# Windowed attention softmax over 128 merged columns in a three-stage float32 kernel

## The chip, the core and the metric

The kernel runs on one core of one Trainium2 chip. The metric is the device time of one execution in microseconds (us). The engines are TensorE (PE; PEld is its weight load), VectorE (DVE), ScalarE (ACT), GpSimd (POOL) and SyncE (SP), which here only issues DMAs.

## The reference, cut to what matters

Attention over 2 batches, 8 heads, 576 positions of 64 numbers, with a causal window of 128 keys; its output, as 1152 tokens of 512 numbers, goes through a layer of four experts and then through a second network with a cosine in it.

```python
rel = pos[:, None] - pos[None, :]
bias = slopes[:, None, None] * (-np.abs(rel).astype(np.float32))[None, :, :]
mask = (rel >= 0) & (rel < 128)
scores = np.where(mask, scale * np.matmul(q, k.transpose(0, 1, 3, 2)) + bias[None], -1000000000.0)
attn = np.exp(scores - np.max(scores, axis=-1, keepdims=True))
attn = attn / (np.sum(attn, axis=-1, keepdims=True) + 1e-09)
x = np.matmul(attn, v)                      # then laid out as [1152, 512]
for e in range(4):                          # p: domain_probs over their sum
    out += p[:, e:e + 1] * (np.maximum(x @ w1[e], 0.0) @ w2[e])
h = out @ w_in
return (h * np.cos(h)) @ w_out
```

## The kernel before

The order of all instructions on each engine is written out by hand: loops in Python yield pieces, and the pieces are queued in the order in which the loops call them. Each engine takes its own queue strictly in that order.

**Attention** comes first. A unit is a batch and a block of queries (one of 64, four of 128); `attention` takes each unit in two halves of four heads, so there are 20 steps, numbered k = 0 to 19. Step k queues the scores of its own half (`att_scores`: TensorE into `s_ps`, a VectorE add, scale and minimum per head at L358, a ScalarE exponential per head at L363), the reciprocal of step k-1 (`att_sums`, with a GpSimd add of 1e-9 at L372), one job of `weights()`, the transposes of step k-3 with the two copies `pt` out of PSUM (L411 VectorE, L413 ScalarE), the normalisation of step k-1 on GpSimd (L379), and the products with the values of step k-4 (L429, into `x_ps`). After a second half the result is split into a high and a low part on ScalarE and VectorE. A query block sees its own 128 keys and the 128 of the block ahead, so scores, exponentials and normalisation run over 256 columns, of which the mask `bm` leaves 128. From step 12 on, matmuls of the first layer (`plain`, L561) are put between. Jobs of `weights()` split the weights of the next group of 512 hidden features into a high part (ScalarE, L155 and L184) and a low part (GpSimd, L130).

**Groups** follow: eight for the experts, four for the second network. A group is two `pair` products (L533), `layer2` products (L627) and four `plain` products for the next group. Between them `run` calls `jobs`, `advance` (the cosine and its split), `cv` (which converts the second network's weights, given as 8-byte words, through `cr` and `cv` tiles at L224 to L251) and `move` (which makes the seven transformed operands of the pair products out of the tokens, `transform`). In the last expert group (`turn`) the results are transposed (`flip`, named f0 to f8) to become the second network's input.

At the very start four matmuls on zeros (`WARM`, L683) run while the first keys are on their way. The keys of the first batch lie in the tile `xk`, whose first part later becomes `xf`.

Of the kernel before, what the change touches and what calls it, by code (L numbers as in the profile page):

```python
# [49 lines left out]
def tile_kernel(ctx, tc, qT, kT, v, probs, w1, w2, w_in, w_out, out):  # L50
# [21 lines left out]
    ptp = ap("ptp", bufs=4)  # L72
# [7 lines left out]
    scr = ppool.tile([128, 4, 256], F32, name="scr", tag="p")  # L80
    bm = mkp.tile([128, H, 256], BF16, name="bm")

    def constants():
        rel_i, rel, msk = scr[:, 0].bitcast(I32), scr[:, 1], scr[:, 2]
        nc.gpsimd.iota(rel_i, pattern=[[-1, 256]], base=WIN, channel_multiplier=1)
        nc.vector.tensor_copy(rel, rel_i)
        nc.gpsimd.memset(msk, 0.0)
        big = -8.0e9
        nc.gpsimd.affine_select(
            out=msk, in_=msk, pattern=[[-1, 256]], compare_op=ALU.is_ge, fill=big,  # L90
            base=WIN, channel_multiplier=1,
        )
# [5 lines left out]
        for h in range(H):
            slope = 2.0 ** (-8.0 * (h + 1) / H)
            nc.vector.scalar_tensor_tensor(  # L100
                out=bm[:, h, :], in0=rel, scalar=-8.0 * slope, in1=msk,
                op0=ALU.mult, op1=ALU.add,
            )
        make_identity(nc, ident)


    k_t, q_t, v_t = {}, {}, {}

    def load_unit(b, i):
# [13 lines left out]
        q_t[b, i], v_t[b, i] = qt, vt  # L123

# [23 lines left out]
    def weights():  # L148
# [17 lines left out]
        def first_sums(g, j):  # L166

            raw, w = raws[j], w_t[1, g, j]
            a11, a12 = raw[:, 0:2, 0:128], raw[:, 2:4, 0:128]
            a21, a22 = raw[:, 0:2, 128:256], raw[:, 2:4, 128:256]  # L170
            sm = ssp.tile([128, 4, 2, 128], F32, name="sm", tag="sm")
            nc.gpsimd.tensor_tensor(out=sm[:, 0], in0=a21, in1=a22, op=ALU.add)
            sub(nc.gpsimd, sm[:, 1], sm[:, 0], a11)
            sub(nc.gpsimd, sm[:, 2], a11, a21)
            sub(nc.gpsimd, sm[:, 3], a12, sm[:, 1])
            loads_ahead()
            yield
            yield from two_parts(nc.gpsimd, w[:, 0, 1], w[:, 1, 1], sm.rearrange("p s m f -> p (s m f)"))
# [156 lines left out]

    def att_scores(u, g):
# [15 lines left out]
        den = stp.tile([128, 4], F32, name="den", tag="den")
        rec = stp.tile([128, 4], F32, name="rec", tag="rec")
        for m in range(2):
            for hh in range(2):
# [3 lines left out]
                    out=p[:n, k, :wid], in0=ps[hh][:n, m, :wid], in1=bm[:n, h, c0 : c0 + wid],  # L359
# [4 lines left out]
                    out=p[:n, k, :wid], in_=p[:n, k, :wid], func=AF.Exp, scale=-1.0,  # L364
                    bias=nmax[:n, k : k + 1], accum_out=den[:n, k : k + 1],
                )
        state[u, g] = p, den, rec, wid

    def att_sums(u, g):
        n = UNITS[u[1]][1]  # L370
        p, den, rec, wid = state[u, g]
        nc.gpsimd.tensor_scalar(out=den[:n], in0=den[:n], scalar1=1e-9, scalar2=None, op0=ALU.add)  # L372
        nc.vector.reciprocal(out=rec[:n], in_=den[:n])  # L373

    def att_normalise(u, g):
        n = UNITS[u[1]][1]
        p, den, rec, wid = state[u, g]
        for s in (slice(0, 2), slice(2, 4)):
            nc.gpsimd.tensor_tensor(  # L379
                out=p[:n, s, :wid], in0=p[:n, s, :wid],  # L380
                in1=rec[:n, s].unsqueeze(2).to_broadcast([n, 2, wid]), op=ALU.mult,
            )
        state[u, g] = p

    def key_blocks(i):
        o = 0
        for j in ([i - 1] if i else []) + [i]:
            yield j, o, UNITS[j][1]
            o += UNITS[j][1]

    def att_transpose(u, g):
        p = state[u, g]
        n = UNITS[u[1]][1]
        blocks = list(key_blocks(u[1]))
        pT = []
        for m in range(2):
            tp = ps_t.tile([128, 2, 2, 128], F32, name="t_ps", tag="t_ps")
            pt = ptp.tile([128, 2, 2, 128], F32, name="pt", tag="pt")
            for bi, (j, o, ln) in enumerate(blocks):
                for hh in range(2):  # L400
                    nc.tensor.transpose(  # L401
                        tp[:ln, bi, hh, :n], p[:n, 2 * m + hh, o : o + ln], ident[:n, :n]
                    )
            lens = [ln for j, o, ln in blocks]
            if len(set(lens)) == 1:
                sl = [(slice(0, lens[0]), slice(0, len(blocks)))]
            else:
                sl = [(slice(0, lens[k]), slice(k, k + 1)) for k in range(2)]
            for a, bb in sl:
                if m == 0:  # L410
                    nc.vector.tensor_copy(pt[a, bb, :, :n], tp[a, bb, :, :n])  # L411
                else:
                    nc.scalar.activation(out=pt[a, bb, :, :n], in_=tp[a, bb, :, :n], func=AF.Copy)  # L413
            pT.append(pt)
        state[u, g] = pT

    def att_pv(u, g):
        b, i = u
        s0, n = UNITS[i]
        pT = state.pop((u, g))  # L420
        blocks = list(key_blocks(i))
# [3 lines left out]
        for m in range(2):  # L425
            for bi, (j, o, ln) in enumerate(blocks):
                for hh in range(2):
                    h = 4 * g + 2 * m + hh
                    nc.tensor.matmul(  # L429
                        xt[64 * hh : 64 * hh + 64, 2 * g + m, :n],  # L430
                        v_t[b, j][:ln, 64 * h : 64 * h + 64],
                        pT[m][:ln, bi, hh, :n],
                        start=(bi == 0), stop=(bi == len(blocks) - 1),
                    )
# [243 lines left out]
    with tc.manual_schedule():  # L678

        warm = ppool.tile([128, 4, 256], F32, name="warm", tag="p")  # L680
        nc.vector.memset(warm[:, 0], 0.0)
        for _ in range(WARM):
            nc.tensor.matmul(  # L683
                ps1.tile([128, 512], F32, name="o_ps", tag="o_ps")[:, :256],
                warm[:, 0, :128], warm[:, 0], start=True, stop=True,
# [5 lines left out]
        def fill(k, s):  # L691
# [7 lines left out]
            if s == 0 and 4 <= k < 18:  # L699
# [26 lines left out]
    def steps(g):  # L726
# [17 lines left out]
        if g > 0:  # L744
            yield layer2(g, 1), 2, 2 * turn, 2
# [5 lines left out]
        njobs = 0 if last else 2 if turn else 5 if early else 9  # L751
        if g == 0:
            njobs += 1
        for k, o in enumerate(order):
            more = min(njobs, 2 if g == 0 and k == 0 else 1)
            if isinstance(o, int):
                assert not any(c > 0 for c, _ in chains)
                yield layer2(g, o), 2, more, 2 if k in (1, 4, 7) else 1 if k < 9 else 0
# [3 lines left out]
            elif not last:  # L762
                yield plain(g + 1, int(o[1])), 2, more, 2
            njobs -= more

    def run(groups):
        for g in groups:
            for step, stages, njobs, ncv in steps(g):
                next(step)
                for _ in range(stages):  # L770
# [5 lines left out]
                move(2)  # L776
# [7 lines left out]
    with tc.manual_schedule():  # L784
        run(range(NG1 - 1))
# [45 lines left out]
```

## Time and profile before

| | us |
|---|---|
| median of 3 runs | 676.09 (674.96 to 679.61) |
| the profiled execution | 675.06 |
| its span, first to last instruction | 673.3 |
| TensorE busy in the span | 648.1 |
| VectorE, GpSimd, ScalarE busy | 420.4, 372.4, 336.7 |

The span leaves 1.76 us of the execution outside. Busy times are sums over stages that differ, so they only tell which engine has little room on the whole.

### The profile page before, as it was taken

Reading aid. Unit: us, or ns where it says so; the run is one execution under the profiler, and the core shown is the slowest. Engines: PE = TensorE matmul, PEld = TensorE weight load, DVE = VectorE, ACT = ScalarE, POOL = GpSimd, SP = SyncE. Lnnn points to the kernel's source line nnn. Section 1 sums busy time; section 2 is a strip of 40 time slices with the busy share of each in tenths; the row PEclk is TensorE's granted clock in tenths of the full one; section 3 lists DMA queues with packets and bytes.
Section 4 is the critical chain, followed back from the end, with each engine's and each line's share of the span. In section 5 each row is a group of like instructions: output and inputs, shape, how many; then the busy total and the mean of one; then the engine's idle time right before and its main releaser. Section 6 shows DMA issues by size and latency. Waiting matters only on the chain.

```text
span 673.3 us, 9797 instructions
## 1 busy us (share of the span) xinstructions
PE 648.1 (96%) x3516; PEld 569.5 (85%) x3516; DVE 420.4 (62%) x821; ACT 336.7 (50%) x768; POOL 372.4 (55%) x376
## 2 busy tenths in 40 slices
PE   8879999979999999999999999999899999999997
PEld 5667789878898898998998998988788998998976
DVE  5645674587866858659669663455675464564562
ACT  6868744245334334344343251246675675675660
POOL 3987737517538147357166174194458749649540
PEclk7989999999999999999999999999999999999999
DMA  8135101553625504526325322011001200201002
GB/s 259 40 121 164 32 1 34 183 159 87 198 76 156 173 32 156 173 57 207 104 102 202 126 48 78 32 63 33 1 32 33 77 17 32 93 2 47 34 31 93
DMA packets 39728, 60.41 MB, mean 90 GB/s; under 512 B 5632, under 2 KB 22016, under 8 KB 39680
## 3 DMA queue, kind: packets, MB, share of 16 engines
q1 hardware_dynamic: 39680, 59.80, 27.7%
q8 instruction: 27, 0.44, 0.3%
q14 instruction: 21, 0.17, 0.1%
HBM read 49.04 MB, written 10.75 MB: 89 GB/s over the span
## 4 chain that ended last, share of the span: by engine, by line
PE 75%; DVE 8%; ACT 6%; POOL 5%; issue 3%; DMA 2%; SPq 0%; ACTq 0%; DVEq 0%; POOLq 0%
PE o_ps L627 38%; PE o_ps L533 20%; PE o_ps L561 13%; POOL p L379 2%; DVE u L505 2%; ACT r L503 2%; PE s_ps L346 2%; DMA cr<-w_in 2%; ACT u L502 2%; PE x_ps L429 2%; POOL hpair L130 1%; PE t_ps L401 1%; DVE o_ps L576 1%; DVE u L511 1%; DVE c L576 1%
## 5 line engine op out<-in xcount | busy, mean ns | idle before, releaser
L627 PE MATMUL o_ps<-w2t,hpair 128*128 128x512 f32 x864 | 207.2, 392 | 1.2 <-POOL hpair L130 1.0
L627 PEld LDWEIGHTS o_ps<-w2t,hpair 128*128 128x128 f32 x864 | 160.7, 188 | 35.1 <-POOL hpair L130 2.3
L533 PE MATMUL o_ps<-xs,w1t 128*128 128x384 f32 x1008 | 182.3, 336 | 8.3 <-ACT p L582 3.0
L533 PEld LDWEIGHTS o_ps<-xs,w1t 128*128 128x128 f32 x1008 | 175.4, 188 | 13.7 <-ACT p L582 3.9
L130 POOL TENSOR_TENSOR w1t<-raw,w1t 128x512 fp32r<-128x512 f32 x48 | 66.1, 1390 | 95.3 <-ACT w1t L155 95.2
L130 POOL TENSOR_TENSOR w2t<-raw,w2t 128x512 fp32r<-128x512 f32 x48 | 62.4, 1312 | 90.0 <-ACT w2t L184 88.7
L561 PE MATMUL o_ps<-xq,w1t 128*128 128x384 f32 x576 | 110.3, 338 | 0.0
L561 PEld LDWEIGHTS o_ps<-xq,w1t 128*128 128x128 f32 x576 | 101.6, 188 | 3.3
L627 PE MATMUL o_ps<-w2t,h 128*128 128x512 f32 x432 | 103.3, 392 | 0.0
L627 PEld LDWEIGHTS o_ps<-w2t,h 128*128 128x128 f32 x432 | 80.5, 188 | 16.1 <-issue 0.2
L505 DVE SCALAR_TENSOR_TENSOR u<-r,u 128x384 f32<-128x384 f32 x48 | 38.7, 810 | 57.8 <-ACT r L503 57.8
L130 POOL TENSOR_TENSOR w1t<-sm,w1t 128x512 fp32r<-128x512 f32 x48 | 67.2, 1416 | 7.4 <-ACT w1t L155 7.3
L130 POOL TENSOR_TENSOR hpair<-u,hpair 128x384 fp32r<-128x384 f32 x32 | 32.6, 1039 | 42.5 <-ACT hpair L513 42.5
L155 ACT ACTIVATE w1t<-sm 128x512 fp32r<-128x512 f32 x48 | 30.3, 631 | 45.7 <-POOL sm L130 45.7
L521 DVE SCALAR_TENSOR_TENSOR hpair<-o_ps,hpair 128x384 fp32r<-128x384 f32 x48 | 26.7, 556 | 33.1 <-ACT hpair L520 33.1
L363 ACT ACTIVATE p<-p,nmax 128x256 f32<-128x256 f32 (+2 forms) x80 | 36.3, 455 | 17.0 <-DVE nmax L358 17.0
L232 ACT ACTIVATE cr<-cr 128x512 int32<-128x512 uint32 x32 | 21.6, 675 | 44.6 <-DMA cr<-w_in 30.9
L520 ACT ACTIVATE hpair<-o_ps 128x384 fp32r<-128x384 f32 x48 | 23.4, 488 | 40.2 <-DVE o_ps L576 39.5
L244 ACT ACTIVATE cr<-cr 128x512 f32<-128x512 f32 x32 | 21.7, 679 | 38.9 <-DVE cv L238 38.9
L642 DVE SCALAR_TENSOR_TENSOR accpair<-o_ps,pr,accpair 128x512 f32<-128x512 f32 x42 | 31.0, 744 | 12.5 <-PE o_ps L627 12.5
L379 POOL TENSOR_TENSOR p<-p,rec 128x512 f32<-128x512 f32 (+2 forms) x40 | 34.1, 872 | 5.6 <-DVE rec L373 5.6
L234 DVE TENSOR_SCALAR cv<-cr 128x512 int32<-128x512 int32 x32 | 21.7, 678 | 24.6 <-DMA cr<-w_in 20.8
(99 smaller groups left out, 826.9 us busy)
## 6 DMA issues: line engine op xcount, KB each, us to landing
raw<-w SPq DMA_DIRECT2D x32, 512.0 KB, 3.9
cr<-w_in SPq DMA_DIRECT2D x16, 512.0 KB, 5.0
cr<-w_out SPq DMA_DIRECT2D x16, 512.0 KB, 4.2
wi<-cv SPq DMA_DIRECT2D x16, 256.0 KB, 4.4
wo<-cv SPq DMA_DIRECT2D x16, 256.0 KB, 2.3
raw<-wi SPq DMA_DIRECT2D x8, 512.0 KB, 3.4
raw<-wo SPq DMA_DIRECT2D x8, 512.0 KB, 3.6
qt<-qT SPq DMA_DIRECT2D x8, 256.0 KB, 4.3
```

What stands on the lines that cost most here:

```text
L130: eng.tensor_tensor(out=out, in0=a, in1=b, op=ALU.subtract)
L155: nc.scalar.activation(out=hi[:, s], in_=src[:, s], func=AF.Copy)
L234: nc.vector.tensor_scalar(out=o, in0=hw, scalar1=3, scalar2=0x3FFFFFF8, op0=ALU.logical_shift_left, op1=ALU.bitwise_and,)
L363: nc.scalar.activation(out=p[:n, k, :wid], in_=p[:n, k, :wid], func=AF.Exp, scale=-1.0, bias=nmax[:n, k : k + 1], accum_out=den[:n, k : k ...
L379: nc.gpsimd.tensor_tensor(out=p[:n, s, :wid], in0=p[:n, s, :wid], in1=rec[:n, s].unsqueeze(2).to_broadcast([n, 2, wid]), op=ALU.mult,)
L505: nc.vector.scalar_tensor_tensor(out=u, in0=r, scalar=MAGIC, in1=u, op0=ALU.subtract, op1=ALU.subtract)
L520: nc.scalar.activation(out=hi, in_=src, func=AF.Relu)
L521: nc.vector.scalar_tensor_tensor(out=lo, in0=src, scalar=0.0, in1=hi.bitcast(F32), op0=ALU.max, op1=ALU.subtract)
L533: nc.tensor.matmul(ps, w(a, k, m), xs[:, bb, b, m], start=(start and m == 0 and (a, bb) == PASSES[0]), stop=(stop and m == 1 and (a, bb) = ...
L561: nc.tensor.matmul(ps, w(a, 2 * (q % 2) + d // 2, d % 2), xq[:, bb, d], start=(d == 0 and (a, bb) == PASSES[0]), stop=(d == ND - 1 and (a, ...
L627: nc.tensor.matmul(ps, h0[:, a, f, t * 128 : (t + 1) * 128] if t < NQ else hpair[:, a, f, (t - NQ) * 128 : (t - NQ + 1) * 128], w_t[2, g, ...
L642: nc.vector.scalar_tensor_tensor(out=o, in0=ps, scalar=s, in1=o, op0=ALU.mult, op1=ALU.add)
```

## The change

For a query in row r of a block, column j of the block's own keys is allowed where j is at most r, and column j of the block ahead where j is greater than r. The two sets never meet, so one set of 128 columns holds both: a predicated copy (the mask `later` is 128.0 where j > r) puts the scores of the block ahead over those of the own block, in PSUM. Minimum, exponential, normalisation and transposes then run over 128 columns. The product needs the values of the right block in each place: it is made as all weights times the values ahead, plus the weights of own columns (`po`, the transposed weights times the mask `own`) times the difference of the two blocks' values (`vd`, one GpSimd subtraction per unit). The 1e-9 lies beside each sum in a tile `dens`, and VectorE adds the two (L413). The zeros for the first matmuls move into the tile that takes the keys. In the groups, conversion, job and transform pieces are called at other places, and `P2` of the turn is cut into two halves with `f8` between them.

```diff
-    scr = ppool.tile([128, 4, 256], F32, name="scr", tag="p")
-    bm = mkp.tile([128, H, 256], BF16, name="bm")
+    later = mkp.tile([128, 2, 128], F32, name="later")
+    own = mkp.tile([128, 128], F32, name="own")
+    va = mkp.tile([128, DM], F32, name="va")
+    bm = mkp.tile([128, 2, H, 128], BF16, name="bm")
...
+        if i == 1:
+
+            nc.sync.dma_start(out=va[64:], in_=v[b, :64, :])
+
+    def values(b, i):
+
+        ahead = va if i == 1 else v_t[b, i - 1]
+        vd = vdp.tile([128, DM], F32, name="vd", tag="vd")
+        nc.gpsimd.tensor_tensor(out=vd, in0=v_t[b, i], in1=ahead, op=ALU.subtract)
+        v_d[b, i] = ahead, vd
...
             nc.gpsimd.tensor_tensor(out=sm[:, 0], in0=a21, in1=a22, op=ALU.add)
             sub(nc.gpsimd, sm[:, 1], sm[:, 0], a11)
+            yield
...
         next(gens[0])
+        yield
...
+        if i:
+            for hh in range(2):
+                nc.vector.copy_predicated(
+                    ps[hh][:n, :, 128 + c0 :], later.bitcast(U32)[:n, :, c0:], ps[hh][:n, :, c0:128]
+                )
         for m in range(2):
             for hh in range(2):
                 k = 2 * m + hh
                 h = 4 * g + k
                 nc.vector.tensor_tensor_reduce(
-                    out=p[:n, k, :wid], in0=ps[hh][:n, m, :wid], in1=bm[:n, h, c0 : c0 + wid],
+                    out=p[:n, k, :n], in0=ps[hh][:n, m, 128 : 128 + n], in1=bm[:n, int(i > 1), h, :n],
                     scale=-0.125, scalar=3.0e38, op0=ALU.add, op1=ALU.min,
                     accum_out=nmax[:n, k : k + 1],
                 )
...
-        nc.gpsimd.tensor_scalar(out=den[:n], in0=den[:n], scalar1=1e-9, scalar2=None, op0=ALU.add)
-        nc.vector.reciprocal(out=rec[:n], in_=den[:n])
+        nc.vector.tensor_reduce(out=rec[:n], in_=den[:n], axis=mybir.AxisListType.X, op=ALU.add)
+        nc.vector.reciprocal(out=rec[:n], in_=rec[:n])
...
-        for s in (slice(0, 2), slice(2, 4)):
-            nc.gpsimd.tensor_tensor(
-                out=p[:n, s, :wid], in0=p[:n, s, :wid],
-                in1=rec[:n, s].unsqueeze(2).to_broadcast([n, 2, wid]), op=ALU.mult,
-            )
+        nc.gpsimd.tensor_tensor(
+            out=p[:n, :, :n], in0=p[:n, :, :n],
+            in1=rec[:n].unsqueeze(2).to_broadcast([n, 4, n]), op=ALU.mult,
+        )
         state[u, g] = p
...
+        if g == 0 and u[1]:
+            values(*u)
...
-        for m in range(2):
-            tp = ps_t.tile([128, 2, 2, 128], F32, name="t_ps", tag="t_ps")
-            pt = ptp.tile([128, 2, 2, 128], F32, name="pt", tag="pt")
...
-                if m == 0:
-                    nc.vector.tensor_copy(pt[a, bb, :, :n], tp[a, bb, :, :n])
-                else:
-                    nc.scalar.activation(out=pt[a, bb, :, :n], in_=tp[a, bb, :, :n], func=AF.Copy)
...
+        tp = ps_t.tile([128, 4, 128], F32, name="t_ps", tag="t_ps")
+        for k in range(4):
+            nc.tensor.transpose(tp[:n, k, :n], p[:n, k, :n], ident[:n, :n])
+        pt = ptp.tile([128, 4, 128], F32, name="pt", tag="pt")
+        nc.scalar.activation(out=pt[:n, :, :n], in_=tp[:n, :, :n], func=AF.Copy)
+        po = None
+        if u[1]:
+            po = ptp.tile([128, 4, 128], F32, name="po", tag="po")
+            nc.vector.tensor_tensor(
+                out=po, in0=tp, in1=own.unsqueeze(1).to_broadcast([128, 4, 128]), op=ALU.mult
+            )
+        state[u, g] = pt, po
...
+                ahead, more = v_d[u]
+                nc.tensor.matmul(o, ahead[:, hs], pt[:, k], start=True, stop=False)
+                nc.tensor.matmul(o, more[:, hs], po[:, k], start=False, stop=True)
...
-        warm = ppool.tile([128, 4, 256], F32, name="warm", tag="p")
-        nc.vector.memset(warm[:, 0], 0.0)
+        warm = xf[:, 0:2]
+        nc.vector.memset(warm, 0.0)
+        nc.vector.memset(dens, 1e-9)
...
-            if s == 0 and 4 <= k < 18:
+            if s == 0 and 4 <= k < 20:
                 next(jobs)
...
-            ("f1", 3, "f2", 6, "f3", "P0", "f6", 4, "P1", 7, "f4", 5, "f7", 8, "f5", "P2", "f8", "P3") if turn else
+            ("f1", 3, "f2", 6, "f3", "P0", "f6", 4, "P1", 7, "f4", 5, "f7", 8, "f5", "P2a", "f8", "P2b", "P3") if turn else
...
-                yield layer2(g, o), 2, more, 2 if k in (1, 4, 7) else 1 if k < 9 else 0
+                yield layer2(g, o), 2, more, 2 if k < 7 else 1 if k < 9 else 0
...
                 next(step)
+                move(2)
                 for _ in range(stages):
                     advance()
                 for _ in range(njobs):
                     next(jobs)
                 for _ in range(ncv):
                     next(cv, None)
-                move(2)
...
     with tc.manual_schedule():
+        next(cv)
         run(range(NG1 - 1))
```

What the order of instructions shows at three places. First SyncE's queue at the start of the program; `qt`, `xk` and `vt` are queries, keys and values of units 0 and 1. Before:

```order
L120 DMA qt<-qT 128x4x64
L121 DMA xk<-kT 128x4x64
L122 DMA vt<-v 64x512
L120 DMA qt<-qT 128x512
L121 DMA xk<-kT 128x4x128
```

And now:

```order
L143 DMA qt<-qT 128x4x64
L144 DMA xk<-kT 128x4x64 [waits DVE_49,PE_49]
L145 DMA vt<-v 64x512
L143 DMA qt<-qT 128x512
L144 DMA xk<-kT 128x4x128
```

The first load of keys now waits for a VectorE and a TensorE instruction, those on the zeros, and every later load stands behind it.

Second, VectorE at the end of step 17 and the beginning of step 18; L520 and L521, later L548 and L549, make the hidden features `h`. Before:

```order
L358 ISA p,nmax<-s_ps,bm 128x256
L358 ISA nmax 128x1
L373 RECIPROCAL rec<-den 128x4 [waits Activation_49,Pool_49]
L411 COPY pt<-t_ps 128x512 [waits DVE_49,PE_49]
L521 SCALAR_TENSOR_TENSOR h_127<-o_ps,h_127 128x384 [waits Activation_49]
L358 ISA p,nmax<-s_ps,bm 128x256 [waits PE_49]
```

And now:

```order
L413 TENSOR_REDUCE rec<-dens 128x4
L414 RECIPROCAL rec<-rec 128x4 [waits DVE_49]
L438 TENSOR_TENSOR po<-t_ps,own 128x512 [waits Activation_49]
L549 SCALAR_TENSOR_TENSOR h_134<-o_ps,h_134 128x384 [waits Activation_49]
L392 COPY_PREDICATED s_ps<-later,s_ps 128x2x128 [waits PE_49] x2
L399 ISA p,nmax<-s_ps,bm 128x128 [waits DVE_49,Pool_49]
```

The copy that waited for TensorE has become a product that waits for ScalarE: for the copy `pt` out of the same `t_ps` (L434), which on ScalarE's queue stands behind step 17's four exponentials and its job, as L413 did before. Two predicated copies stand ahead of the next step's first reduction.

Third, SyncE's queue at the first conversions; `raw` are weights of the groups, `wi` is the converted result on its way out. Before:

```order
L145 DMA raw<-w 128x4x256 [waits DMAHW0_49,DMAHW5_49,Activation_49,Pool_49]
L145 DMA raw<-w 128x2x512 [waits DMAHW6_49,DMAHW4_49,Pool_49]
L224 DMA cr<-w_in 128x1024 [waits DMAHW7_49,DVE_49,PE_49]
L224 DMA cr<-w_in 128x1024
L145 DMA raw<-w 128x4x256 [waits DMAHW1_49,DMAHW5_49,Activation_49,Pool_49]
L251 DMA wi_120<-cv 128x512 [waits DMAHW2_49,DVE_49]
L224 DMA cr<-w_in 128x1024 [waits DMAHW7_49,DMAHW3_49,Activation_49]
```

And now:

```order
L258 DMA cr<-w_in 128x1024 [waits DVE_49,DMAHW7_49,PE_49,Pool_49]
L178 DMA raw<-w 128x4x256 [waits DMAHW0_49,DMAHW5_49,Activation_49,Pool_49]
L178 DMA raw<-w 128x2x512 [waits DMAHW6_49,DMAHW1_49,Pool_49]
L258 DMA cr<-w_in 128x1024 [waits DMAHW2_49]
L285 DMA wi_126<-cv 128x512 [waits DMAHW3_49,DVE_49]
L258 DMA cr<-w_in 128x1024 [waits DMAHW7_49,DMAHW4_49,Activation_49]
L178 DMA raw<-w 128x4x256 [waits DMAHW0_49,Pool_49]
```

The first `cr` load has moved ahead of two weight loads, and the third ahead of one.

## Rows read from the trace of the kernel before

**Rows 1.** Windows by stage: busy us (instructions) of each engine, TensorE clock, DMA share.
```profile
0.00:94.30 94.30, 82.72 (x684) 62.88 (x685) 57.93 (x249) 66.80 (x231) 66.29 (x97) 0.93 0.36 110
...
94.30:150.00 55.70, 52.16 (x269) 47.45 (x268) 35.30 (x58) 21.14 (x43) 25.27 (x23) 1.00 0.33 105
...
455.00:500.00 45.00, 40.45 (x214) 35.72 (x212) 29.28 (x54) 30.39 (x70) 20.97 (x22) 1.00 0.08 24
```

**Rows 2.** The chain that ended last, in order of time: start, us, what.
```profile
2.96 4.30 DMA xk<-kT
...
20.89 2.04 POOL p L379 x2
...
46.46 0.63 PE t_ps L401 x4
```

**Rows 3.** Timeline, ScalarE and VectorE in attention step 17: start, us, instruction.
```profile
65.88 0.42 DVE L358 CUSTOM_DVE_ANT_0 p<-s_ps,bm 128x256 f32<-128x256 f32 x1 [1.16 <-PE s_ps L346]
...
66.23 0.42 DVE L358 CUSTOM_DVE_ANT_0 p<-s_ps,bm 128x256 f32<-128x256 f32 x1
...
66.40 0.51 ACT L363 ACTIVATE p<-p,nmax 128x256 f32<-128x256 f32 x1 [1.02 <-DVE nmax L358]
...
68.39 0.61 ACT L184 ACTIVATE w2t<-raw 128x512 fp32r<-128x512 f32 x1
...
68.91 0.57 ACT L413 ACTIVATE pt<-t_ps 128x512 f32<-128x512 f32 x1
...
69.89 0.56 DVE L521 SCALAR_TENSOR_TENSOR h<-o_ps,h 128x384 fp32r<-128x384 f32 x1 [0.59 <-ACT h L520]
...
70.48 0.42 DVE L358 CUSTOM_DVE_ANT_0 p<-s_ps,bm 128x256 f32<-128x256 f32 x1
```

**Rows 4.** Groups by form, 0 to 120 us: busy us, mean ns of one.
```profile
L363 ACT ACTIVATE p<-p,nmax 64x64 f32<-64x64 f32 x16 | 5.4, 335 | 6.4 <-DVE nmax L358 6.4
...
L130 DVE TENSOR_TENSOR xq<-x_ps,xq 128x512 fp32r<-128x512 f32 x2 | 1.4, 681 | 0.0
...
L358 DVE CUSTOM_DVE_ANT_0 p<-s_ps,bm 64x64 f32<-64x64 f32 x16 | 2.6, 211 | 0.4 <-PE s_ps L346 0.3
...
L411 DVE COPY pt<-t_ps 128x256 f32<-128x256 f32 x4 | 1.6, 406 | 0.0
```

**Rows 5.** Timeline, TensorE in attention step 18.
```profile
69.32 1.14 PE L346 MATMUL s_ps<-kt,qt 64*128 64x256 f32 x8
...
70.38 1.09 PE L401 MATMUL t_ps<-ident,p 128*128 128x128 f32 x8
...
72.45 1.09 PE L429 MATMUL x_ps<-pt,vt 128*64 128x128 f32 x16
```

**Rows 6.** Timeline of the start: SyncE (SPq) and TensorE.
```profile
1.21 0.49 SPq L121 DMA_DIRECT2D xk<-kT  x1
...
1.17 3.78 PE L683 MATMUL o_ps<-warm 128*128 128x256 f32 x8 [1.17 <-DVE warm L681]
...
4.88 0.56 PE L346 MATMUL s_ps<-xk,qt 64*64 64x64 f32 x10
```

**Rows 7.** Timeline, VectorE: first score reduction of steps 5 and 19.
```profile
16.41 0.42 DVE L358 CUSTOM_DVE_ANT_0 p<-s_ps,bm 128x256 f32<-128x256 f32 x1 [1.24 <-PE s_ps L346]
...
74.64 0.42 DVE L358 CUSTOM_DVE_ANT_0 p<-s_ps,bm 128x256 f32<-128x256 f32 x1 [1.18 <-PE s_ps L346]
```

**Rows 8.** Windows before and in a fall of the TensorE clock (columns as Rows 1).
```profile
34.90:37.70 2.80, 0.00 (x0) 0.02 (x1) 0.90 (x3) 1.36 (x3) 2.64 (x4) 1.00 0.59 204
...
39.00:42.60 3.60, 3.33 (x31) 2.84 (x28) 1.33 (x10) 2.93 (x15) 3.44 (x5) 0.53 0.25 79
```

**Rows 9.** Timeline, SyncE and VectorE at the first weight conversions.
```profile
129.49 0.37 SPq L224 DMA_DIRECT2D cr<-w_in  x1
...
135.61 0.43 DVE L234 TENSOR_SCALAR cv<-cr 128x512 int32<-128x512 int32 x1 [4.94 <-DMA cr<-w_in]
```

**Rows 10.** Timeline, TensorE at the turn between the two networks.
```profile
479.70 5.98 PE L533 MATMUL o_ps<-xs,w1t 128*128 128x384 f32 x30 [2.04 <-ACT xs L276]
```

More of the change, by code (lines that the diff above doesn't have):

```diff
@@ new lines, in tile_kernel @@
+    own = mkp.tile([128, 128], F32, name="own")
+    va = mkp.tile([128, DM], F32, name="va")
+    bm = mkp.tile([128, 2, H, 128], BF16, name="bm")
+    def constants():
+        rel_i = own.bitcast(I32)
+        nc.gpsimd.iota(rel_i, pattern=[[-1, 128]], base=0, channel_multiplier=1)
+        nc.gpsimd.memset(later, 0.0)
+        nc.gpsimd.affine_select(
+            out=later, in_=later, pattern=[[0, 2], [-1, 128]], compare_op=ALU.is_ge, fill=float(WIN),
+            base=0, channel_multiplier=1,
+        )
@@ new lines, in constants @@
+        for e in range(2):
+            for h in range(H):
+                slope = 2.0 ** (-8.0 * (h + 1) / H)
+                if e == 0:
+                    nc.vector.scalar_tensor_tensor(
+                        out=bm[:, e, h], in0=rel, scalar=-8.0 * slope, in1=edge,
+                        op0=ALU.mult, op1=ALU.add,
+                    )
+                else:
+                    nc.gpsimd.tensor_scalar(
+                        out=bm[:, e, h], in0=rel, scalar1=-8.0 * slope, scalar2=None, op0=ALU.mult
+                    )
+            if e == 0:
+                make_identity(nc, ident)
@@ L93, in constants @@
+        nc.gpsimd.memset(va[:64], 0.0)
+        nc.gpsimd.memset(own, 1.0)
         nc.gpsimd.affine_select(
-            out=msk, in_=msk, pattern=[[1, 256]], compare_op=ALU.is_ge, fill=big,
-            base=-1, channel_multiplier=-1,
-        )
[L98 to L102, printed above, removed]
-            )
@@ L104, in constants @@
-        make_identity(nc, ident)
-    k_t, q_t, v_t = {}, {}, {}
+            out=own, in_=own, pattern=[[1, 128]], compare_op=ALU.is_ge, fill=0.0,
+            base=0, channel_multiplier=-1,
+        )
+    k_t, q_t, v_t, v_d = {}, {}, {}, {}
     def load_unit(b, i):
@@ L334, in tile_kernel @@
     state, xps = {}, {}
+    dens = mkp.tile([128, 4, 4, 2], F32, name="dens")
     def att_scores(u, g):
@@ L425, in att_pv @@
         for m in range(2):
[L426 to L434, printed above, removed]
+            for hh in range(2):
+                k = 2 * m + hh
+                h = 4 * g + k
+                hs = slice(64 * h, 64 * h + 64)
+                o = xt[64 * hh : 64 * hh + 64, 2 * g + m, :n]
+                if i == 0:
+                    nc.tensor.matmul(o, v_t[u][:n, hs], pt[:n, k, :n], start=True, stop=True)
+                    continue
+                ahead, more = v_d[u]
+                nc.tensor.matmul(o, ahead[:, hs], pt[:, k], start=True, stop=False)
+                nc.tensor.matmul(o, more[:, hs], po[:, k], start=False, stop=True)
         if g == 1:
@@ L684, in tile_kernel @@
                 ps1.tile([128, 512], F32, name="o_ps", tag="o_ps")[:, :256],
-                warm[:, 0, :128], warm[:, 0], start=True, stop=True,
+                warm[:, 0, :128], warm[:, 1, :256], start=True, stop=True,
             )
@@ L762, in steps, with half @@
             elif not last:
-                yield plain(g + 1, int(o[1])), 2, more, 2
-            njobs -= more
+                if len(o) < 3:
+                    yield plain(g + 1, int(o[1])), 2, more, 2 if k < 7 else 1
+                else:
+                    if o[2] == "a":
+                        halved = plain(g + 1, int(o[1]), True)
+                    yield half(halved, o[2] == "b"), 1, 0, 0
+            njobs -= more
+    def half(step, end):
+        next(step)
+        yield
+        if end:
+            whole(step)
     def run(groups):
```

65 lines of the change are left out of this document (23 added, 42 removed).

## The prediction

> **What bounds the kernel now.** I read the windows by stage first: TensorE is busy 648 of 673.3 us in all, but idle 11.6 us in the attention (82.72 of 94.30), 3.54 us in the stretch in which the first conversions of the second network's weights fall, and 4.55 us at the turn between the networks [rows 1]. Only in these three can the change give or take time; elsewhere TensorE has hardly a gap.
>
> The chain in order of time says what bounds the attention [rows 2]. It begins with the 4.30 us landing of the keys of unit 1, issued at 2.96. From 16.4 to 46.4 it runs along GpSimd's normalisations (2.04 us for the two of a step); from 46.46 it runs along TensorE, between whose pieces first-layer matmuls now stand. So up to about step 12 the attention's pace is set by other engines, and after it by a mix.
>
> The timeline of step 17 shows how little room VectorE and ScalarE have between them [rows 3]. A reduction starts 0.35 after the one before; the first exponential starts 0.52 after the first reduction (0.10 after its end); four exponentials take 1.99, the weights' job 0.52 and the copy `pt` 0.57; then come VectorE's `h` and the next step, 4.60 after this one began. TensorE's own step 18 runs from 69.32 to about 73.5: scores 1.14, eight transposes and their waits up to 72.45, products 1.09 [rows 5].
>
> **The change part by part**, against the profiled execution (675.06: the span and 1.76 around it; 1.0 under the median).
>
> *The start: +4.0 (3.2 to 4.5).* The zeros now lie in the tile that takes the keys, so the first key load waits for all warm matmuls. It was issued at 1.21, while these ran from 1.17 for 3.78 [rows 6]; it can now be issued at some 5.45 (4.95 and a hop). SyncE takes its queue in order, so every load behind it moves too: unit 1's keys were issued 1.75 after the first load, now 7.2, and with 4.30 of landing [rows 2] they are there at 11.5 instead of 7.26. I take 4.0, as a little slack stands between landing and use; 3.2 holds if the steps up to 5, with less work on GpSimd, catch up.
>
> *The attention's loop, step 5 to step 19: +0.5.* What is saved looks large: four of eight transposes (0.42 of TensorE's step at full clock), one of two normalisations (1.02 of GpSimd's 2.04), half the columns of four reductions and four exponentials. But a new wait ties the steps together. `po` on VectorE reads the same `t_ps` as ScalarE's `pt`, and the order makes it wait for `pt`, which stands behind the four exponentials and the job of the same step. Behind `po` on VectorE stand `h` and then the predicated copies and the reductions of the next step, on which ScalarE's next exponentials hang. So a step is now a closed ring; its parts, with prices from rows:
> - Two predicated copies of 128x2x128. No such operation is in the trace. The rows give 0.21 for a 64x64 reduction and 0.406 for a copy of 128x256 out of PSUM [rows 4]; it has two inputs in PSUM, or 256 elements as the copy, so I take 0.34 each, 0.68. Ends: half that, and twice that.
> - From the first reduction to the first exponential 0.38: a 128-column reduction of 0.28 (between 0.21 for 64 columns and 0.42 for 256) and the 0.10 of before.
> - Four exponentials of 128 columns: 0.335 each for 64 [rows 4], 1.99/4 = 0.50 for 256 [rows 3]; 0.39 between, 1.56.
> - The job 0.52 and `pt` 0.57, both as before [rows 3].
> - `po`, 128x512 out of PSUM with a second input: between the 0.57 of ScalarE's `pt` of that size [rows 3] and the 0.68 of VectorE's `xq<-x_ps` [rows 4]; I take 0.61.
>
> The sum is 4.32. Every odd step adds 0.59 for `h`, or for the low part of the transformed tokens [rows 3, 4]: 4.91. Steps 8, 9, 12 and 13 lack the job on ScalarE, the 64-row blocks are shorter, and step 14 is bound by TensorE. That gives 4 x 4.91 (steps 5, 7, 15, 17) + 3 x 4.32 (6, 16, 18) + 15.49 (8, 9, 12, 13) + 7.05 (10, 11) + 3.60 (14) = 58.74, against 58.23 between the first reductions of steps 5 and 19 [rows 7]. GpSimd (1.02 less per step, some 1.3 more per unit for `vd`) and TensorE (4.2 - 0.42, some 3.75 in a full step) then lie beside the ring, and what they save shows as idle time. After step 19 two remaining transposes save 0.84, and `po` ahead of the tokens' transform costs about as much: 0.
>
> The Trainium skill ("PSUM — Partial Sum Buffer", section "PSUM bank collisions raise a hardware error ⚠️") says that two engines must not touch one PSUM bank at once, reads against reads included; by it the wait is one that cannot be left out, while the two copies of before read different tiles side by side. No run here shows such an error, and the sum rests on the order alone.
>
> *The 1e-9 on VectorE: 0.* A GpSimd instruction and its crossing go, a short VectorE reduce comes; both lie behind the reductions while ScalarE is still at its exponentials. Without that cover it is some 0.2 per step (as a 64x64 reduction [rows 4]). The new constants and masks are GpSimd's before the first normalisation, under the wait for keys: 0.
>
> *The first conversions: -3.2 (-3.5 to 0).* VectorE stood 4.94 us for a `cr` load issued only at 129.49 [rows 9], and with it what TensorE needed. That load now stands ahead of one weight load and the first one ahead of two, and converting starts before the groups. That removes TensorE's 3.54 of idle time [rows 1] but for some 0.3 that I leave for the first load, which still waits for GpSimd. Nothing is gained if `cr` lands no earlier, behind the result `wi` on its way out.
>
> *The turn: -1.3 (-3.5 to 0).* Of the 4.55 idle there [rows 1], 2.04 is one wait for a transformed operand `xs` on ScalarE [rows 10]. Transforms are now queued ahead of the cosines, and the last `flip` lies before the second half of `P2`, some 1.05 earlier (its matmuls cover it). I take 1.3 of the 2.04 and nothing of the rest, which hangs on the cosines.
>
> Sum: 4.0 + 0.5 - 3.2 - 1.3 = 0.0, that is 675.06; I forecast **675**. The terms' bounds give 3.2 - 3.7 - 3.5 - 3.5 = -7.5 to 4.5 + 7 + 0 + 0 = +11.5 (loop: copies at half and twice their price in about 11 full steps), which all at one end is unlikely.
>
> **The rivals.**
> 1. *Faster: the ring does not close.* If VectorE in fact runs a step ahead, the steps fall to the floors of GpSimd and TensorE, nine of about 3.3 (before step 14) and five of 3.75 (8 transposes made 4) = 48.5, or 9.7 less than 58.23: 675 - 0.5 - 9.7 = about **665**. For it: the chain ran along GpSimd and its work halves [rows 2]. Against it: the order, in which `po` stands between two steps on VectorE. Chance 0.18.
> 2. *Slower: the predicated copy is dear.* It reads and writes the same PSUM tile under a mask. At twice the price, 0.68 more in each of about 11 full steps on the ring, it adds 7: **682**. It decides from about 0.65 each. For it: no row shows the operation. Against it: all VectorE rows of this size lie at 0.2 to 0.45 [rows 4]. Chance 0.15.
> 3. *Slower: TensorE's clock falls.* Before, after 2.80 us without a matmul at clock 1.00, a stretch followed at 0.53, that is 1.2 GHz instead of 2.4 [rows 8]. Now TensorE, busy some 2.5 of 4.3 to 4.9 in steps 5 to 11, waits about 2 in each, and some 3 after the warm matmuls. At half rate its step would be 5.2 (3.9 in steps 10 and 11), so these seven take 33.8 instead of 29.4: +4.4, **679.5**. It decides if the waits are long enough to keep the clock down. Against it: at full clock in the other half of the attention first-layer matmuls fill the gaps. Chance 0.15. The Trainium skill ("TensorE: Matmul & The Clock Gate", section "HAM oscillation — how this bites in real kernels") says that waits recurring each turn of a loop can slow the clock each turn; the one fall above agrees, and by that rule this rival would be the likeliest.
>
> **How the numbers follow.** The main case has 0.52. About 1%, 6.8 us, is what a measurement of this kernel can tell from no change. Faster by more (under 669) is rival 1 with most of its spread, and the end of the main case in which the turn and the copies give all: 0.22. Slower by more (over 683) is the upper half of rival 2, or 2 and 3 together, or 3 with a start and conversions that give nothing: 0.15. Within 1%: 0.63. The range 667 to 682 takes in the main case, rival 3 and half of each of the other two.
>
> **What would show it.** The first key load at about 5.4 and unit 1's scores past 11; `po` starting right behind `pt` in each step, and first reductions 4.3 and 4.9 apart in turn; predicated copies of 0.34; a granted clock near 1.00 from 20 to 50 us; no TensorE gap above 1 us between 94 and 150, and one gap fewer at the turn. The forecast is wrong if the wait of `po` is short, if the copy's duration is off by half, or if the clock stays down in the attention.

## The result, and the profile after

The changed kernel took **680.75 us** (median of 9 runs, 679.98 to 681.45) against 676.19 before (9 runs, 674.96 to 679.61): a ratio of 1.0059, 95% interval 1.0044 to 1.0074. It is 0.6% slower. That lies inside the range of 667 to 682, but it is clear of no change, and the forecast of 675 was next to no change. The profiled span is 678.6 us against 673.3.

Four marks that both programs have (three first pieces of a run of matmuls, and the last run of 64) divide the difference of 5.2 to 5.3 us. First the chain in order of time of the kernel before (start, us, what; the line at 7.40 is the scores of unit 1):

```profile
7.40 0.94 PE s_ps L346 x8
...
109.08 2.08 PE o_ps L561 x12
...
155.87 5.48 PE o_ps L627 x24
...
500.59 5.48 PE o_ps L627 x24
...
654.84 14.86 PE o_ps L627 x64
```

And the chain of the changed kernel, with pieces of its attention that answer to [rows 2], and with the first reductions of steps 5 and 19 (`p` L399 at 22.41 and 79.09):

```profile
7.23 3.71 DMA xk<-kT
11.07 1.67 PE s_ps L382 x8
...
22.41 0.28 DVE p L399
...
31.86 1.39 PE s_ps L382 x8
...
71.09 0.96 ACT p L404 x5
...
73.08 0.69 DVE po L438
...
79.09 0.29 DVE p L399
...
114.85 2.08 PE o_ps L589 x12
...
157.10 5.48 PE o_ps L655 x24
...
503.63 5.48 PE o_ps L655 x24
...
660.06 14.81 PE o_ps L655 x64
```

Where the chain of before ran along GpSimd and TensorE, it now runs through the exponentials on ScalarE and `po` on VectorE. With these two reductions (before: [rows 7]) the account is:

| stretch | forecast, us | profiles, us |
|---|---|---|
| to the first reduction of step 5 | +4.0 | 22.41 - 16.41 = +6.0 |
| steps 5 to 19 | +0.5 | 56.68 - 58.23 = -1.55 |
| step 19 to the first mark | 0 | 35.76 - 34.44 = +1.3 |
| first to second mark, conversions | -3.2 | 42.25 - 46.79 = -4.5 |
| second to third mark, with the turn | -1.3 | 346.53 - 344.72 = +1.8 |
| third to last mark, second network | not named | 156.43 - 154.25 = +2.2 |
| sum | 0.0 | +5.2 |

The windows of the changed kernel at the conversions and at the turn, which answer to [rows 1]:

```profile
94.30:150.00 55.70, 55.65 (x307) 50.61 (x306) 43.84 (x69) 24.65 (x52) 27.62 (x26) 1.00 0.36 114
455.00:500.00 45.00, 40.58 (x201) 36.13 (x200) 28.35 (x53) 30.34 (x68) 21.35 (x22) 0.92 0.08 24
```

TensorE's idle time at the conversions is gone (0.05 of 55.70). At the turn there are still 4.42 us, and the clock is now 0.92.

Windows of fixed times compare the same work only where it has not moved, so for the rest they go from mark to mark. First the kernel before (the start to the first mark, the second mark to the third, the third to the last), then the changed one:

```profile
0.00:109.08 109.08, 97.50 (x769) 77.62 (x770) 68.44 (x266) 72.17 (x242) 72.05 (x103) 0.94 0.31 95
155.87:500.59 344.72, 340.18 (x1717) 306.30 (x1717) 231.69 (x362) 150.35 (x295) 173.84 (x157) 1.00 0.33 104
500.59:654.84 154.25, 152.35 (x753) 135.19 (x752) 87.22 (x141) 95.78 (x197) 102.93 (x99) 1.00 0.12 38
```

```profile
0.00:114.85 114.85, 98.17 (x705) 77.06 (x706) 73.23 (x314) 66.41 (x239) 67.56 (x83) 0.97 0.33 97
157.10:503.63 346.53, 342.11 (x1718) 308.95 (x1717) 237.05 (x361) 150.87 (x295) 174.96 (x155) 0.99 0.33 104
503.63:660.06 156.43, 152.31 (x753) 135.11 (x752) 82.50 (x140) 95.21 (x196) 101.37 (x98) 1.00 0.11 37
```

Up to the first mark GpSimd and ScalarE have 4.5 and 5.8 us less to do and TensorE 64 matmuls fewer, but VectorE has 4.8 more, TensorE's busy time is no shorter, and the stretch is 5.8 longer. From the second mark to the third TensorE idles as long as before (4.42 for 4.54) but takes 1.9 longer over the same matmuls. Behind the third mark it is as busy as before and idles 2.2 longer.

**The ring.** The timeline of step 17, ScalarE and VectorE, which answers to [rows 3]:

```profile
70.07 0.28 DVE L399 CUSTOM_DVE_ANT_0 p<-s_ps,bm 128x128 f32<-128x128 f32 x1
...
70.40 0.40 ACT L404 ACTIVATE p<-p,nmax 128x128 f32<-128x128 f32 x1 [1.63 <-DVE nmax L399]
...
71.96 0.61 ACT L218 ACTIVATE w2t<-raw 128x512 fp32r<-128x512 f32 x1
72.47 0.57 ACT L434 ACTIVATE pt<-t_ps 128x512 f32<-128x512 f32 x1
...
73.08 0.69 DVE L438 TENSOR_TENSOR po<-t_ps,own 128x512 f32<-128x512 f32 x1 [1.80 <-ACT pt L434]
...
73.69 0.55 DVE L549 SCALAR_TENSOR_TENSOR h<-o_ps,h 128x384 fp32r<-128x384 f32 x1
...
74.16 0.75 DVE L392 COPY_PREDICATED s_ps<-later,s_ps 128x256 f32<-128x256 uint32 x2
74.81 0.28 DVE L399 CUSTOM_DVE_ANT_0 p<-s_ps,bm 128x128 f32<-128x128 f32 x1
```

VectorE stands 1.80 us for `pt`, then does `po`, `h` and the two copies before the next step's reduction; ScalarE had stood 1.63 for this step's reduction in the same way. Link by link: 0.33 to the first exponential, 1.56 for the four, 0.51 for the job, 0.61 for `pt`, 0.61 `po`, 0.47 `h`, 0.65 the copies: 4.74, where 4.91 was forecast. Steps 15 to 18 are 4.74, 4.28, 4.74 and 4.28 long; before they were 4.89, 4.42, 4.60 and 4.16, so that the lighter steps gain nothing here.

**The start.** Timeline of SyncE and TensorE, answering to [rows 6]:

```profile
5.59 0.38 SPq L144 DMA_DIRECT2D xk<-kT  x1
...
8.00 0.87 PE L382 MATMUL s_ps<-xk,qt 64*64 64x64 f32 x10 [2.44 <-DMA xk<-kT]
```

The load is issued at 5.59 instead of 1.21, and unit 1's scores start at 11.07 instead of 7.40. That is 3.7, near the 4.0 of the forecast; the other 2.3 of this stretch come behind it. By form (mean ns of one), TensorE's scores from 12 to 24 us and from 60 to 80 us:

```profile
L382 PE MATMUL s_ps<-xk,qt 64*128 64x256 f32 x18 | 6.7, 687 | 0.3 <-DVE nmax L399 0.3
...
L382 PE MATMUL s_ps<-kt,qt 64*128 64x256 f32 x36 | 6.6, 402 | 0.0
```

From the first scores to about 27 us TensorE's matmuls run slowly, after 2.44 us without any; before, the slow stretch ended at 18.6 (granted clock 0.52 from 8 to 18.6).

**After step 19.** TensorE, and what it waits for on VectorE in the changed kernel:

```profile
82.10 0.69 DVE L438 TENSOR_TENSOR po<-t_ps,own 128x512 f32<-128x512 f32 x1 [1.80 <-ACT pt L434]
...
83.96 0.41 DVE L163 TENSOR_TENSOR xk<-x_ps,xk 128x256 f32<-128x256 f32 x1
...
84.48 0.45 PE L461 MATMUL x_ps<-pt,vt 128*64 128x128 f32 x4 [4.10 <-issue]
```

The next products go into `x_ps`, which VectorE's last reading of it frees at 84.37; it stands behind `po` and three more instructions. Before, TensorE was idle there for 1.24:

```profile
79.97 1.09 PE L429 MATMUL x_ps<-pt,vt 128*64 128x128 f32 x16 [1.24 <-ACT xs L276]
```

The granted clock of the changed kernel then falls:

```profile
84.70:88.60 3.90, 3.90 (x25) 3.24 (x22) 3.83 (x7) 2.10 (x6) 3.17 (x4) 0.56 0.31 118
```

**The second network.** GpSimd and TensorE in group 9 of the changed kernel:

```profile
560.38 1.28 POOL L163 TENSOR_TENSOR w1t<-raw,w1t 128x512 fp32r<-128x512 f32 x1
561.62 2.29 POOL L163 TENSOR_TENSOR hpair<-u,hpair 128x384 fp32r<-128x384 f32 x2
...
562.67 2.55 PE L655 MATMUL o_ps<-w2t,hpair 128*128 128x512 f32 x10 [1.37 <-POOL hpair L163]
```

A weights' job of 1.28 us stands between GpSimd's low parts of the features, and TensorE waits 1.37 for the one behind it. Before, four of these ran in a row and the same place cost 0.19:

```profile
555.44 3.99 POOL L130 TENSOR_TENSOR hpair<-u,hpair 128x384 fp32r<-128x384 f32 x4 [4.80 <-ACT hpair L513]
...
558.51 3.74 PE L627 MATMUL o_ps<-w2t,hpair 128*128 128x512 f32 x15 [0.19 <-POOL hpair L130]
```

### The profile page after: what moved, and what is told of

It reads as the page before. It is cut to its first block, busy times and chain, and to the rows that moved or that the text cites. A ratio compares the mean times of both kernels' runs of the same rounds, so it can differ in the third digit from the quotient of the medians.

```text
span 678.6 us, 9665 instructions
## 1 busy us (share of the span) xinstructions
PE 649.6 (96%) x3452; PEld 571.8 (84%) x3452; DVE 429.4 (63%) x867; ACT 331.3 (49%) x764; POOL 369.0 (54%) x356
## 4 chain that ended last, share of the span: by engine, by line
PE 76%; DVE 10%; ACT 10%; issue 2%; POOL 1%; DMA 1%; SPq 0%; DVEq 0%; ACTq 0%; POOLq 0%
PE o_ps L655 38%; PE o_ps L561 20%; PE o_ps L589 13%; ACT p L404 2%; PE s_ps L382 2%; DVE u L533 2%; ACT r L531 1%; ACT u L530 1%; DVE xs L163 1%; DVE po L438 1%; ACT pt L434 1%; ACT xs L311 1%; DVE o_ps L604 1%; DVE u L539 1%; POOL hpair L163 1%
## 5 line engine op out<-in xcount | busy, mean ns | idle before, releaser
L561 PEld LDWEIGHTS o_ps<-xs,w1t 128*128 128x128 f32 x1008 | 177.2, 189 | 8.1 <-DVE c L604 3.4
L163 POOL TENSOR_TENSOR w2t<-raw,w2t 128x512 fp32r<-128x512 f32 x48 | 66.1, 1394 | 83.8 <-ACT w2t L218 80.6
L655 PE MATMUL o_ps<-w2t,h 128*128 128x512 f32 x432 | 105.0, 396 | 0.0
L655 PEld LDWEIGHTS o_ps<-w2t,h 128*128 128x128 f32 x432 | 82.0, 191 | 16.5 <-issue 0.2
L163 POOL TENSOR_TENSOR w1t<-sm,w1t 128x512 fp32r<-128x512 f32 x48 | 64.5, 1355 | 45.8 <-ACT w1t L188 39.7
L533 DVE SCALAR_TENSOR_TENSOR u<-r,u 128x384 f32<-128x384 f32 x48 | 34.3, 717 | 51.9 <-ACT r L531 51.8
L404 ACT ACTIVATE p<-p,nmax 128x128 f32<-128x128 f32 (+1 forms) x80 | 30.3, 379 | 29.4 <-DVE nmax L399 29.4
L548 ACT ACTIVATE hpair<-o_ps 128x384 fp32r<-128x384 f32 x48 | 23.4, 488 | 36.6 <-DVE o_ps L604 35.9
L549 DVE SCALAR_TENSOR_TENSOR hpair<-o_ps,hpair 128x384 fp32r<-128x384 f32 x48 | 26.6, 555 | 20.3 <-ACT hpair L548 20.3
L272 DVE SCALAR_TENSOR_TENSOR cv<-cr,cv 128x512 int32<-128x512 int32 x32 | 33.1, 1033 | 1.1
L537 ACT ACTIVATE u<-u 128x384 f32<-128x384 f32 x48 | 24.8, 517 | 15.4 <-DVE u L533 15.4
```

Of the source, the lines that this page charges most:

```text
L163: eng.tensor_tensor(out=out, in0=a, in1=b, op=ALU.subtract)
L272: nc.vector.scalar_tensor_tensor(out=a, in0=hw, scalar=-0x40000000, in1=o, op0=ALU.bitwise_and, op1=ALU.bitwise_or,)
L404: nc.scalar.activation(out=p[:n, k, :n], in_=p[:n, k, :n], func=AF.Exp, scale=-1.0, bias=nmax[:n, k : k + 1], accum_out=den[:n, k, 0:1],)
L533: nc.vector.scalar_tensor_tensor(out=u, in0=r, scalar=MAGIC, in1=u, op0=ALU.subtract, op1=ALU.subtract)
L537: nc.scalar.activation(out=u, in_=u, func=AF.Sin, scale=-TWOPI)
L548: nc.scalar.activation(out=hi, in_=src, func=AF.Relu)
```

## The experiments

Each was run with the kernel before on the same chip; its medians there were 675.98 (runs 1 to 4), 676.15 (5 to 8) and 676.78 (9 to 11).

**1 and 2. The two parts apart.** Run 1 has the changed attention with `jobs`, `converts`, `fill`, `steps` and `run` of before; run 2 the reverse. The core of run 2:

```diff
+                move(2)
                 for _ in range(stages):
                     advance()
...
-                move(2)
...
+        next(cv)
         run(range(NG1 - 1))
```

> The change's attention with the groups' calls (jobs, conversions, transforms, turn) as they were before. By the account of the two profiles (first reduction of step 5 is 6.0 us later than before, steps 5 to 19 are 1.55 shorter, the stretch from step 19 to the first block of 30 matmuls is 1.3 longer) it is 5.8 slower than before, some 682.0. Rival: the conversions of before waited on loads that are issued by the clock of the weights, and take up a later attention; then it is 2 to 4 slower, 678 to 680.

> The attention of before with only the groups' part of the change. By the account (conversions -4.5, turn +1.8 with its fall of TensorE's clock, a job ahead of the features in two groups of the second network +2.2) it is 0.5 faster than before, 675.7. Rival: the fall of the clock at the turn is an accident of when the attention ends, and without it the turn gives the 1.3 that was forecast; then 3.6 faster, 672.6.

Measured: 681.78, ratio 1.0097 (1.0082 to 1.0112), and 676.20, ratio 1.0001 (0.9981 to 1.0021). Both are what the account gives. The attention is the whole loss. The groups' part gives 3.5 us of waits at the conversions (none is left in run 2 from 94 to 165 us) and takes as much back. The waits of run 2 on TensorE from 495 to 615 us (us in total, times, longest) show a part of where:

```profile
PE o_ps L629 <- POOL hpair L130: 3.7, 3, 1.4
```

There are three such waits, not two: in the changed kernel the first was covered by a turn that took longer. The profiled execution of run 2 is the fastest of its ten (673.46), and the clock did not fall at its turn, so its trace shows no loss there; where the others, up to 4.6 us slower, lost more is not shown.

**3. Zeros in a tile of their own.**

```diff
-        warm = xf[:, 0:2]
-        nc.vector.memset(warm, 0.0)
+        warm = ppool.tile([128, 4, 128], F32, name="warm", tag="p")
+        nc.vector.memset(warm[:, 0:2], 0.0)
...
-                warm[:, 0, :128], warm[:, 1, :256], start=True, stop=True,
+                warm[:, 0], warm[:, 0:2], start=True, stop=True,
```

> The whole change, but the zeros of the first matmuls in a tile of their own, so that the first key load waits for nothing. If late keys are the whole cost of the start and bring the long stretch of slow matmuls with them: first scores at 5, step 5 at 16.5 instead of 22.4, and 6 us faster than the change, 674.7. Rival: TensorE's matmuls fall to half rate after the first scores anyway, as before from 8 to 18.7 us; then only the 3.3 to 3.7 of the late keys come back, 677.

Measured: 676.00, ratio 0.9997 (0.9978 to 1.0016), 4.75 under the change; between the 674.7 expected and the rival's 677. The first scores start at 4.96, step 5 at 18.98 instead of 22.41, which is still 2.6 later than before. TensorE's slow stretch stays, from 8 to 22 us. The profiled execution took 678.01, the slowest of the ten, so its trace cannot show all of the 4.75.

**4. `po` before `pt`.** In `att_transpose` the two calls change places, so that ScalarE's copy waits for VectorE's product.

> The whole change, but po (VectorE) reads the transposes first and pt (ScalarE) waits for po, so that VectorE no longer waits for the exponentials of its own step. If the ring of the two engines sets the pace: steps 15 to 19, 4.74 and 4.28 apart in the change, fall to TensorE's 3.8 to 4.0, and po no longer stands late ahead of the last transforms; 4 to 6 us faster than the change, 675 to 677. Rival: the steps are paced by TensorE's slow stretches and by x_ps, which the next unit's products wait for; then under 1.5 us faster, over 679.

Measured: 674.79, ratio 0.9993 (0.9976 to 1.0011), 5.96 under the change. Steps 15 to 18 are 4.51, 2.37, 4.69 and 3.17 long (mean 3.69 against 4.51), and TensorE's wait behind step 19 falls from 4.10 to 2.58. Of step 17 in this run VectorE's piece, without a wait:

```profile
66.56 0.66 DVE L437 TENSOR_TENSOR po<-t_ps,own 128x512 f32<-128x512 f32 x1
```

The ring was the pace of the steps, and it was the order of two readers of one tile that closed it.

**5. The job behind the features.**

```diff
-            yield layer2(g, 1), 2, 2 if turn else int(not last), 2
+            yield layer2(g, 1), 2, 2 if turn else int(early), 2
...
-        njobs = 0 if last else 4 if turn else 6 if early else 10
+        njobs = 0 if last else 4 if turn else 6 if early else 11
...
-            more = min(njobs, 2 if g == 0 and k < 2 else 1)
+            more = min(njobs, 2 if g == 0 and k < 2 or not early and k == 3 else 1)
```

> The whole change, but in the second network's groups the weights' job that now comes with the second layer's product 1 is put three pieces later, behind GpSimd's low parts of the hidden features. If that job ahead of hpair is what TensorE waits for (1.37 and 1.40 us in two groups), both waits go: 2.2 to 2.8 us faster than the change, 678.2. Rival: the cosine chain ends as late anyway and the wait stays with another releaser; then under 0.7 faster.

Measured: 677.87, ratio 1.0023 (1.0010 to 1.0036), 2.9 under the change. TensorE's waits for `hpair` from 495 to 640 us:

```profile
PE o_ps L655 <- POOL hpair L163: 0.3, 2, 0.2
```

**6. Fillers at the start.** Run 3 and, in step k below 4, matmuls of constants (`ident`, `later`) into an `o_ps` that nobody reads: 2, 7, 3 and 3.

> As the run with zeros in a tile of their own, and with 15 more matmuls of 128x256 on constants that nobody reads, in steps 0 to 3, where TensorE waited. If TensorE's half rate from 8.4 to 22 us is what makes the steps 2 to 6 take 2.7 to 4.6 us, and the waits ahead of it bring it on: the granted clock stays at 1.00, step 5 starts 2 to 4 us sooner than in that run, and the time is 672 to 674 against its 676.0. Rival: the rate falls all the same, or the steps wait for the loads and the engines' ring; then 676 or up to 1.5 more.

Measured: 677.77, ratio 1.0024 (1.0013 to 1.0036), 1.8 over run 3. As a step to a faster kernel it failed: three of the fillers took 1.56, so the seven pushed step 2 from 9.70 to 11.82. But the window from 8 to 22 us of run 3 (first) and of this run shows what they do:

```profile
8.00:22.00 14.00, 12.98 (x68) 9.04 (x68) 7.14 (x49) 9.16 (x42) 6.58 (x9) 0.52 0.91 257
```

```profile
8.00:22.00 14.00, 12.91 (x92) 9.24 (x90) 7.18 (x51) 9.09 (x44) 6.11 (x8) 1.00 0.91 256
```

The granted clock stays at 1.00 (2.4 GHz) instead of 0.52 (1.2 GHz), the scores of 64x256 take 404 ns there instead of 671, and steps 2 to 5 take 12.31 instead of 13.89. So the waits of TensorE at the start do bring the low clock, and it costs 1.6 us there, all of it in steps 2 to 4. On the ring it costs next to nothing: step 5 is 4.61 in run 3, most of it at the low clock, and 4.60 here.

**7. The three edits of runs 3, 4 and 5 together.**

> The whole change with the three edits at once: zeros in a tile of their own, po ahead of pt, and the job behind the features. If the three costs lie in different places they add up: 680.75 - 4.75 - 5.96 - 2.4 = 667.6. Rival: the first two overlap, as both end in the wait of TensorE at step 19 to 20; then 670 to 672.

Measured: 667.95, ratio 0.9884 (0.9861 to 0.9906). The three costs nearly add up: 13.6 singly, 12.8 together.

**8. The turn in the order of before.** `P2` whole, `f8` behind it, and in that group `move(2)` behind the jobs, in the otherwise changed kernel.

> The whole change, but at the turn the pieces in the order of before: P2 whole, f8 behind it, and transforms behind the cosines. If the two waits that now follow each other there (1.69 and 1.31, with one group of 6 matmuls between) bring the half rate behind them, worth 3.1 us: the waits are as before (2.04 first, then 30 matmuls), the clock stays at 1.00 and the time is 1.5 to 2 us under the change, 679. Rival: the second network's waits for the job take up what is won, as where the clock stayed up with the groups' part alone; then 680 to 680.7.

Measured: 681.30, ratio 1.0080 (1.0059 to 1.0101), no faster. The clock did stay at 1.00 at the turn, but an hpair wait of 0.85 in the group behind it was open again, and with the new distribution of jobs the order of before had a wait of 1.91 for `accpair` where the new order has 0.98. The theory that this order costs something falls.

**9. The 1e-9 on GpSimd**, as before the change, in a `den` tile per step.

> The whole change, but with the 1e-9 added by GpSimd as before (sums in a tile per step, no reduce on VectorE). VectorE's reduce takes 0.15 to 0.16 and starts while ScalarE is still at its exponentials; po waits for those anyway. If that cover holds, nothing: 680.2 to 681.2. Rival: the crossing to GpSimd and back (a wait of 0.4 us and more for the sums, once per step) stands in the ring, as VectorE must have the reciprocal before po; then 2 to 5 us slower, 683 to 686.

Measured: 681.09, ratio 1.0070 (1.0051 to 1.0090), not to be told from the change. Steps 15 to 18 are 4.79, 4.34, 4.80 and 4.34: VectorE's add is worth 0.06 a step.

**10. Run 7 with six fillers** (1, 3, 1 and 1).

> The run with the three edits (zeros in a tile of their own, po first, the job moved), with 6 more matmuls of 128x256 that nobody reads in steps 0 to 3: 1, 3, 1 and 1. In the run with 15 of them these took 0.52 us each, so that step 2 came 2.1 us later, but with the matmuls at full rate steps 2 to 6 took 12.31 instead of 13.89. If the half rate there costs 1.6 us and the fillers fit the waits: 666.0 to 667 against 667.95. Rival: six do not keep the rate up, or the keys of the next units set these steps; then 667.5 to 669.

Measured: **663.53**, ratio 0.9816 (0.9792 to 0.9839), 4.4 under run 7 and faster than both kernels. The window from 8.5 to 22 us of run 7 and of this run:

```profile
8.50:22.00 13.50, 12.47 (x64) 8.46 (x66) 8.25 (x51) 9.11 (x40) 7.50 (x9) 0.52 0.91 259
```

```profile
8.50:22.00 13.50, 11.65 (x96) 7.90 (x92) 10.36 (x64) 10.31 (x46) 9.22 (x10) 1.00 0.94 257
```

Step 19 begins at 65.17 instead of 67.64, so 2.5 of the gain come from here (with the ring open, the clock counts for more than the 1.6 of run 6). Another 1.5 lie between the second mark and the third: in the profile of run 7 the clock fell at the turn, in that of this run it did not. Whether the fillers have a part in this second gain is not shown.

**11. The mended attention alone**: runs 3 and 4 with the groups' calls of before.

> Only the attention of the change, with zeros in a tile of their own and po first, and the groups' calls as they were before. The attention alone stood at 681.78; less the 4.75 and 5.96 of the two edits this is 671.1, 5 us under before, which would be what 128 merged columns are worth once their two waits are gone. Rival: the 4.5 that the conversions took off a late start of the groups is missed here, since an earlier attention meets the same loads; then 673 to 675.

Measured: 673.19, ratio 0.9951 (0.9934 to 0.9967), the rival: TensorE's waits of 1.47 and 2.27 at the conversions are there again.

## Why the prediction was wrong

What failed is the sum of 0.0: two terms of the changed calls were missing or had the wrong sign, and the start was too small. The premise behind it, that only the attention, the conversions and the turn can give or take time, failed in the second network. By the account the terms were off by +2.0, -2.05, +1.3, -1.3, +3.1 and +2.2. That the first four cancel is luck; the turn and the second network are left, 5.3 together.

- **The second network was not in the sum.** The prediction costed the turn and the conversions and let the other groups' calls go; there TensorE now idles 2.2 longer. The job that now comes with `layer2(g, 1)` stands ahead of `hpair` on GpSimd and makes TensorE wait some 1.4 us in two groups of the profile, and 0.9 in a third where a longer turn does not cover it (run 2); moving it gave 2.9 (run 5). It is the kind of moved step for which every queue it passes has to be gone through.
- **The start, "+4.0".** Late keys are 3.7 of it, as worked out. What failed is the spacing of the steps up to 5, which the account left as before: they fell another 2.3 back, in TensorE's slow stretch, which lasted to 27 us. The late keys are not the cause of that, as it stays in run 3; at full clock the same steps are 1.6 shorter (run 6). Undoing the late keys gave 4.75.
- **The loop, "+0.5".** The ring exists, at 4.74 and 4.28 instead of 4.91 and 4.32, and opening it is worth 6 us (run 4). Mis-sized were the steps without a job (14.77 for steps 8, 9, 12 and 13 instead of 15.49) and step 14 (2.71 instead of 3.60). In all 2.05 too much.
- **After step 19, "0".** `po` ahead of the transform costs 2.9 us of TensorE's time more than before, and a fall of the clock behind it; +1.3 was left.
- **The conversions, "-3.2".** The mechanism was right; the first load gave its part too: TensorE's whole 3.5 of waits went, and 4.5 between the marks; what the last 1.0 is was not found.
- **The turn, "-1.3".** The idle sum hardly changed (4.42 for 4.55). The wait of 2.04 [rows 10] went, and its time turned up at the next pieces (1.69 for ScalarE's `p`), probably since the chain of cosines sets the end there (not tested). The +1.8 is the clock, a term that the sum did not have: it fell behind these waits, and 12 matmuls took 4.21 us where runs 5 and 6 have 2.35.

Of the rivals, the first (no ring) is false; with the ring opened, run 4 takes 51.17 us from step 5 to step 19, where this rival had 48.5. The second (a dear copy) is false: two copies take 0.65, where 0.68 was the forecast. The third had the right mechanism in the wrong place: the low clock costs little in the ring, but 1.6 us ahead of step 6 (run 6), and 2.5 by step 19 where the ring is open (run 10). The Trainium skill's rule named there ("TensorE: Matmul & The Clock Gate", section "HAM oscillation — how this bites in real kernels"), that waits recurring in a loop can slow the clock each turn, agrees with the start: there the clock read 0.52, and 1.00 with fillers in the waits. In the ring it did not come each turn: in run 6 steps 6 to 9 had 1.00, 1.00, 0.54 and 1.00.

Not settled: why run 3 gives 4.75 in the medians and only 3.4 by the first reduction of step 5 (its profile is of its slowest execution, with a fall of the clock at the turn); and what makes TensorE's clock fall at the turn (below).

## What to carry to other kernels

Where two engines read one PSUM tile, the order in which they are written decides who waits for whom: put first the reader whose queue holds the next step's work. Work that is taken off three engines saves nothing while a fourth wait closes a ring around them; follow the ring's links before adding up what is saved. When calls are moved between queues, go through every group in which the call now stands, not only those the move was meant for.

## What the hardware showed that was not expected

- The granted clock's record is not always complete: in the profile of the changed kernel it reads 1.00 from 10 to 34 us, while matmuls of 64x256 took 687 ns, against 402 at 60 to 80 us. Durations by form are the check. In run 3, with the same matmuls at 671 ns, it reads 0.52.
- Six matmuls that nobody reads, by an estimate some 3 us of TensorE's time (six times the 0.52 of run 6), kept the clock at 1.00 from 8.5 to 22 us (run 10), where it reads 0.52 without them (run 7).
- At the turn the same instructions ran at either clock in different runs, whose kernels differ elsewhere: 12 matmuls behind the same two waits took 4.21 us in the changed kernel and in run 9, 3.92 in run 3, and 2.35 in runs 5 and 6. What decides it was not found.
